# Gated mix of 32-head attention and a dense layer: 23 dense pieces cut into 92 products of 32 rows, ten more summed sets, and a new order

## The chip, the cores and the metric

The kernel runs on one core of one Trainium2 chip. A core has five engines with queues of their own: TensorE (PE in the profile; its weight loads are listed apart as PEld), VectorE (DVE), ScalarE (ACT), GpSimd (POOL) and SyncE (SP), which here only issues transfers and waits. The metric is the device time of one execution in microseconds (us). A run is also profiled once; the profile's span goes from the first instruction to the last one of that execution.

## The reference

One batch, S = 2048 rows of D = 640. The first half is softmax attention with 32 heads of 20 columns, the second a dense layer with 1536 hidden columns and the Mish activation. A sigmoid gate for each row mixes the two.

```python
qkv = (x @ wqkv)                      # to q, k, v of 32 heads, 20 columns each
scores = einsum("bhqd,bhkd->bhqk", q, k) * 20 ** -0.5
o = einsum("bhqk,bhkd->bhqd", softmax(scores), v)
a = o @ wo                            # heads side by side: 2048 x 640

h = x @ w1 + b1                       # 2048 x 1536
b = (h * tanh(softplus(h))) @ w2      # Mish, 2048 x 640

g = sigmoid((x * gate_w).sum(-1))
out = g * a + (1 - g) * b
```

All inputs are bf16.

## The kernel before

**Attention.** Four heads are worked on together: a head's 20 columns are padded to 32 rows, so four heads fill the 128 rows of the array. There are 8 such passes of four heads and 4 chunks of 512 queries, so 32 groups G; a group has 16 key tiles j of 128 keys. A *score unit* is 128 keys by 512 queries of one head: one matmul of 32 rows by 128 columns (`score`, L1073), in the row group of its head (`tile_position=(32 * t_, 0)`). Consecutive score matmuls are called a *visit* here; those in different row groups run side by side. There are 2048 units. 1380 of them get their exponential on ScalarE (`emit_exp`, L1091), one, two or three units an instruction. The other 668 are 167 *sets* of four units (one key tile, all four heads), whose power of two VectorE builds by a multiply and an add into int16 (`power_of`, L586). From that one power a set makes further summands by adding a constant to the int16 bits, which GpSimd does on four at a time as int64 (L616). Of the 167 sets, 155 have three summands, which PE weights and adds (three PV passes); 12 are *summed* (`two` in `d_take`): GpSimd makes a shifted copy, VectorE adds it to the power (`total`, L640), GpSimd shifts once more, and PE has two passes. A *PV pass* (`emit_pv`, L1108) is four matmuls of 128 rows by 21 columns, one in each column group, side by side, onto one PSUM bank (`acc`). There are 834 passes. After its last pass a group is normalised and stored to `o_dram`, from which blocks are loaded back transposed (`load_o`, L923) for the product with `wo`.

**Dense work.** All other products (x@w1, the hidden layer @w2, q, k, v, o@wo) are `Chain`s. A chain holds one PSUM bank from its first piece to its evacuation by VectorE. A *piece* (`product`, L663) takes 128 rows of the contraction: four matmuls of 128 rows by 32 columns, one in each column group, side by side, with 512, 320 or fewer streamed columns. One chain is open at a time (`chain[0]`).

**Order.** The table `ORDER` (L19 to L296) is written out by hand or by a search: each word is one step, and `steps` (L1294 on) runs them in turn. `S n,bank` issues n scores for ScalarE, `x n` the exponential of n, `d G,T,two` takes a set, `D G,j,r,bank` one unit of a set, `p` a GpSimd shift, `V j,i` a PV pass, `C k,bank` opens chain k, `F` runs its next piece, `y k` the VectorE instruction number k, `m` a Mish over half the hidden layer on ScalarE (L871), `q`, `k`, `o`, `b`, `l` loads. Each word puts an instruction at the end of its engine's queue, so the table sets the order on every engine. SyncE's queue holds, in the order in which the words ran, nearly all transfers: the stores that follow an evacuation, the loads of q, k, b and w1, and the transposing loads of `od`. A transfer stands there with the waits for its data, and with those for the buffer that it writes.

PSUM has 8 banks: 7 for scores and chains, one for `acc`.

Of the kernel before, what the change touches and what calls it, by code (L numbers as in the profile page):

```python
# [9 lines left out]
P = 128  # L10
# [9 lines left out]
S2,4 S2,2 C0,6 S2,0 x2 x2 F F F F F C1,5 F y1 y3 C2,4 F x2 y4 C3,5 S2,2 F x2 y5 C4,4 S2,0 F x2 y2 y6 C6,5 S2,2  # L20
x2 F F F F F F F d2,3,0 F F F F F F F F F F F F F C5,6 F F S2,0 S2,3 F F F x2 y7 d0,6,0 y8 y9 x2 y10 y11 y12
C7,2 F F F F F S2,0 x2 S2,5 C8,3 V0,-1 F F F F F F F F F F F F F F F F F F F F y13 y14 y15 x2 V1,-1 S3,0 C9,4
F F F F F S2,5 x3 x2 y16 d0,8,0 y17 y18 y19 d1,5,0 V2,-1 C10,6 V4,-1 S3,0 S2,3 V3,-1 V5,-1 F F F F F x3 x2 y20
C11,5 F S3,0 F F F F F d1,0,0 F F F F F F F D0,15,3,3 x3 D0,15,0,4 F F F F F F F C12,6 F F S3,0 F F F y21 y23
y24 y25 y26 y27 y22 x3 D0,15,2,5 S2,3 x2 y29 d3,4,0 y28 V6,-1 V7,-1 S3,0 C13,5 F F D0,14,3,6 S2,3 F F F x2 q1
y30 y31 x1 x2 C14,0 F F F V9,-1 D0,15,1,6 S2,1 F F F F F F F F F F F S2,3 D0,14,0,5 F V8,-1 y32 x2 q2 y33 x2
D0,14,1,6 S2,1 F F F F F y34 x2 y35 V10,-1 C15,6 S3,3 y36 y37 y38 y39 F F F F F D0,14,2,2 S2,0 F F F F F v0,0
V11,-1 V15,0 y44 y43 y40 p1,1 x3 x2 D1,15,1,5 S3,2 y41 y42 x3 V14,0 V15,1 y45 D1,15,0,6 y46 S2,0 V12,-1 C16,5
F F F F F F S3,2 D1,15,2,6 F F F F p2,7 p3,1 p4,6 d1,2,0 l0 y47 V14,1 V15,2 x2 x3 S2,0 D1,14,0,6 y48 y49 y50
C17,5 V14,2 V13,-1 D1,15,3,2 S2,3 d2,6,0 x2 y51 l1 F F F d1,1,0 x2 y52 D1,14,1,6 S2,0 F F x2 p5,7 S2,2  # L30
D1,14,2,4 x2 p6,8 y53 y54 y55 y56 l2 V0,-1 V1,-1 S2,0 D1,13,0,6 C18,5 F F S3,2 x2 y58 y57 F F F S2,0 D1,13,1,6
V15,0 V15,1 V15,2 V2,-1 x3 y59 l3 y60 x2 D1,12,0,5 y61 C19,6 S3,2 F F F F F F V3,-1 S2,0 D1,14,3,5 F F F F x3
y62 S3,2 x2 l4 y63 p7,8 y64 q3 x1 x2 V4,-1 V5,-1 V14,0 C21,2 D1,13,3,6 D2,15,0,5 S2,0 F d3,5,0 F F F p8,7 y65
y66 x2 S2,3 D1,13,2,6 l5 y67 V14,1 F x2 S2,0 D1,12,3,5 y68 p9,0 V14,2 V13,0 V6,-1 x2 y69 S3,2 D1,12,2,6 p10,8
y70 x1 l6 x2 V7,-1 C20,2 V13,1 S2,0 D1,12,1,5 y71 x2 F F F F F F F F D2,15,3,6 S3,3 F F V13,2 V8,-1 V12,0
p11,7 y72 x3 l7 p12,8 y73 S2,0 D2,15,1,6 y74 y75 d4,0,0 x2 C22,2 V9,-1 V12,1 F D2,14,0,5 S2,3 F F F F
D2,15,2,6 S2,0 F d2,2,0 F F F F y76 x2 l8 y77 x2 y78 S2,4 D2,14,3,3 y79 x2 V10,-1 C23,6 V12,2 F S2,0 D2,14,1,2
F F V11,-1 y80 p13,7 y81 x2 l9 y82 S2,3 D2,13,0,5 F F F F F S2,0 D2,14,2,2 F F p14,1 x2 y84 x2 y83 y85 V15,2
d2,8,1 S2,3 D2,13,3,5 V0,-1 V15,1 V15,0 S2,0 D2,13,1,2 p15,1 x2 e0 p16,7 d2,3,0 x2 y86 y87 y89 y90 e2 V1,-1
V14,0 V14,1 S2,3 D2,12,0,5 C24,2 F F S2,0 D2,13,2,6 F F x2 y91 x2 D2,12,3,3 S2,4 x2 y92 y93 p17,1 F V2,-1 S2,0  # L40
D2,12,1,6 V3,-1 V13,0 V14,2 y94 x2 p18,6 y95 S2,2 x2 D2,11,0,4 C25,5 V13,1 F S2,0 D2,12,2,6 F F y96 y88 y97 x2
D2,11,3,4 S2,2 F F p19,7 y98 x2 S2,0 D2,11,1,6 y99 x2 y101 C26,5 V13,2 V4,-1 D3,15,0,4 S2,2 F F F S2,0
D2,11,2,6 V6,-1 F y102 x2 D3,15,3,4 S2,2 F V5,-1 y100 x2 y103 y105 x2 p20,-1 q4 S2,0 V7,-1 V12,0 x2 d3,6,0
# [12 lines left out]
y154 x2 D4,12,0,6 S2,1 p36,7 x2 y156 V1,-1 V2,-1 C33,5 F S2,3 D4,14,3,0 x2 V15,2 V15,1 S2,1 D4,12,1,6 F F F F
x2 y151 y157 y150 p37,7 S2,3 D4,13,2,0 V14,0 V3,-1 y158 y159 y160 d4,1,0 x2 D4,11,0,6 S2,1 p38,5 y161 y155 x2
V14,1 C35,0 V4,-1 S2,3 D4,13,3,5 F F y162 x2 D4,11,1,6 S2,1 F d5,3,0 F F p39,2 y163 x2 S2,3 D4,12,2,5 y164
V5,-1 V14,2 p40,7 x2 S2,1 D5,15,0,6 y165 V13,1 V6,-1 y166 x2 D4,12,3,0 y167 S3,3 C36,6 F F F D4,11,2,2 S2,0 F
F x3 p41,8 y168 x2 y169 S3,3 V13,2 d5,0,0 C37,2 V13,0 F F D4,11,3,6 S2,0 F d6,4,0 F F x3 x2 d5,2,0 d5,5,0 y170  # L60
y171 p42,-1 p43,7 S2,3 D5,15,1,5 V7,-1 V11,0 V12,0 x2 y172 y173 p44,8 S3,0 D5,15,3,6 V12,1 D5,15,2,5 S2,3
V11,1 V9,-1 V8,-1 V10,-1 V11,2 y174 y175 x3 p45,6 y176 C38,5 S3,0 D5,14,0,6 F F F F F y178 p46,7 x2 x3 y179
y177 C39,0 S2,3 V15,0 V15,1 V0,-1 D5,14,1,6 S2,1 D5,13,0,5 x2 y180 y181 x2 F F F F F y182 S2,3 D5,14,2,6 y183
x2 S2,1 x2 C40,0 D5,13,1,5 V15,2 V2,-1 V1,-1 F y184 y185 D5,14,3,6 S2,3 F F x2 D5,12,0,5 S2,1 y186 y187 F F
p47,1 x2 y188 V3,-1 C41,5 S2,3 D5,13,2,6 V14,0 d6,6,0 F p48,3 x2 y189 D5,12,1,0 S2,1 F F S2,3 D5,13,3,6 F F
y190 y191 x2 S2,0 D6,15,0,2 V4,-1 V14,1 V13,0 y192 p49,7 x2 y193 S3,3 D5,12,3,6 p50,0 y194 x2 V5,-1 D5,12,2,2
S2,0 x3 y195 V13,1 V14,2 V6,-1 V13,2 D6,14,0,5 C42,6 S3,2 p51,8 F F F F q7 q8 y196 x2 p52,1 x3 S2,0 D6,15,2,5
# [12 lines left out]
p66,5 S2,4 D7,13,1,6 d7,0,0 F F F y243 x2 S2,0 D7,13,3,2 V2,-1 V14,0 k2 k3 p68,1 y244 x2 S2,4 D7,13,2,6 V14,1  # L80
V15,2 d8,4,0 y245 y246 x2 D7,12,0,3 p69,6 y247 S3,0 V3,-1 C52,6 F F F F F x1 v3,0 x2 y249 S3,3 D7,12,3,0 C53,6
# [227 lines left out]
def kernel(  # L309
# [12 lines left out]
    nc = tc.nc  # L322
# [326 lines left out]
    def mm_pieces(n, fn):  # L649
        return [(lambda k=k: fn(k)) for k in range(n)]  # L650
# [746 lines left out]
```

## Time and profile before

| | before |
|---|---|
| time, three runs | 684.00, 684.51, 686.26 us (median 684.51) |
| span of the profiled execution | 681.8 us |
| VectorE, L586 (powers), one | 0.682 us, 668 of them |
| VectorE, L640 (total of a summed set), one | 1.210 us, 12 of them |
| GpSimd, L616 (shift), one | 1.042 us, 334 of them |
| GpSimd idle before L616 | 314.2 us |
| granted TensorE clock, mean of the span | 0.999 |

The profiled execution is 2.7 us under the median of the runs. Nearly every time below comes from the profile, so sums are made against its own span of 681.8 us and then set beside the runs. A row of the list of groups has the line, the engine, what is written and read, the shape, the count, and behind the bar the busy time, the mean of one in ns, and the idle time of that engine ahead of such instructions. In a timeline each row is one instruction or a run of equal ones: start, length, engine, line.

### The profile page before, as it was taken

To read this page: it belongs to the slowest core of one execution; us is meant where nothing else is said; L and a number is where in the kernel's file an instruction comes from. 1 tells how busy PE (TensorE), PEld (TensorE's weight loads), DVE (VectorE), ACT (ScalarE), POOL (GpSimd) and SP (SyncE) were. 2 spreads that over 40 slices of the span, in tenths; PEclk is the share of its full clock that TensorE was granted. 3 is DMA by queue.
4 is the path that set the end of the run, shared out by engine and by line. 5 is a ranking of instruction groups with operands and counts; after the bars stand their busy time and mean duration, and the time that the engine had idled before them with its cause. 6 is when DMAs were issued, how large, how long until landed. Compare 5 with 4: busy or idle time off the path is not lost.

```text
span 681.8 us, 24517 instructions
## 1 busy us (share of the span) xinstructions
PE 672.8 (99%) x10355; PEld 234.2 (34%) x10355; DVE 597.3 (88%) x1033; ACT 666.7 (98%) x692; POOL 354.0 (52%) x349
## 2 busy tenths in 40 slices
PE   8999999999999999999999999999999999999997
PEld 4433333323323443333333222222243333333334
DVE  5689989898999889899888988999999988799896
ACT  6999999999999999999999999999999999999996
POOL 5135446454454535565645654456646654466453
PEclk9999999999999999999999999999999999999999
DMA  8444322213312211111231223221232122131221
GB/s 171 118 89 126 81 43 53 53 38 63 89 26 52 49 44 36 26 35 34 43 97 33 43 53 74 64 55 33 56 92 60 21 48 29 41 66 35 60 87 60
DMA packets 128542, 40.47 MB, mean 59 GB/s; under 512 B 94960, under 2 KB 127872, under 8 KB 128432
## 3 DMA queue, kind: packets, MB, share of 16 engines
q1 hardware_dynamic: 126032, 38.29, 25.5%
q8 instruction: 81, 1.33, 0.9%
q10 hardware_dynamic: 2400, 0.62, 0.4%
q14 instruction: 29, 0.24, 0.1%
HBM read 22.29 MB, written 12.78 MB: 51 GB/s over the span
## 4 chain that ended last, share of the span: by engine, by line
PE 89%; ACT 7%; DVE 2%; issue 1%; POOL 0%; DVEq 0%; ACTq 0%
PE Sp L1108 30%; PE Sp L1073 30%; PE Sp L663 29%; ACT E L1091 5%; ACT big L871 2%; DVE T L586 0%; PE Sp L515 0%; PE Sp L1336 0%; DVE T L1151 0%; DVE ot L1353 0%; PE Sp L1217 0%; PE Sp L1123 0%; ACT L1091 0%; PE Sp L1199 0%; ACT big L966 0%
## 5 line engine op out<-in xcount | busy, mean ns | idle before, releaser
L1091 ACT ACTIVATE E<-Sp 128x1024 bf16<-128x1024 f32 (+2 forms) x674 | 634.7, 1127 | 4.4 <-PE Sp L1073 3.7
L616 POOL INT64_ADD T<-T x334 | 344.1, 1042 | 314.2 <-DVE T L586 208.5
L586 DVE TENSOR_SCALAR T<-Sp 128x512 int16<-128x512 f32 x668 | 440.2, 682 | 56.1 <-PE Sp L1073 45.7
L1073 PE MATMUL Sp<-qT,kT 32*128 32x512 bf16 x2048 | 259.5, 384 | 2.9 <-ACT E L1091 1.0
L1073 PEld LDWEIGHTS <-kT 32*128 32x128 bf16 x2048 | 70.1, 91 | 244.9 <-issue 240.4
L1108 PE MATMUL Sp<-E,VA 128*21 128x512 bf16 x1380 | 128.0, 382 | 0.0
L1108 PE MATMUL Sp<-T,VD 128*21 128x512 bf16 x1288 | 117.9, 382 | 0.1
L663 PE MATMUL Sp<-w_sb,big 128*32 128x320 bf16 x1536 | 72.9, 302 | 0.2 <-DVE T L586 0.2
L663 PE MATMUL Sp<-xT,w1t 128*32 128x512 bf16 x960 | 72.2, 382 | 0.0
L1108 PEld LDWEIGHTS <-VA 128*21 128x21 bf16 x2048 | 43.9, 90 | 57.3 <-issue 48.4
L1108 PE MATMUL Sp<-T,VA 128*21 128x512 bf16 x668 | 63.5, 382 | 0.0
L663 PE MATMUL Sp<-xT,ws 128*32 128x512 bf16 x720 | 52.2, 382 | 0.0
L1108 PEld LDWEIGHTS <-VD 128*21 128x21 bf16 x1288 | 29.8, 90 | 38.6 <-issue 32.6
L663 PEld LDWEIGHTS <-big 128*32 128x32 bf16 x1536 | 32.9, 95 | 29.0 <-issue 21.8
L850 DVE TENSOR_SCALAR big<-Sp,b1f 128x512 bf16<-128x512 f32 x48 | 35.6, 741 | 1.8 <-PE Sp L663 1.2
L663 PE MATMUL Sp<-wv,xT 128*32 128x81 bf16 (+2 forms) x960 | 31.0, 257 | 0.0
L663 PEld LDWEIGHTS <-w1t 128*32 128x32 bf16 x960 | 19.8, 95 | 25.4 <-issue 17.4
L752 DVE CAST st<-Sp 128x512 bf16<-128x512 f32 x36 | 24.5, 681 | 2.6 <-PE Sp L663 2.4
L663 PE MATMUL Sp<-wo_sb,od 128*32 128x320 bf16 (+1 forms) x608 | 26.3, 301 | 0.1
L1137 DVE STREAM_TRANSPOSE T<-Sp 128x512 f32<-128x512 f32 x32 | 22.7, 709 | 2.6 <-PE Sp L1108 2.4
L663 PEld LDWEIGHTS <-xT 128*32 128x32 bf16 x960 | 18.8, 96 | 10.8 <-issue 7.7
L663 PEld LDWEIGHTS <-ws 128*32 128x32 bf16 x720 | 15.3, 95 | 19.4 <-issue 12.1
(76 smaller groups left out, 196.8 us busy)
## 6 DMA issues: line engine op xcount, KB each, us to landing
w1t<-in_B_w_dram SPq DMA_DIRECT2D x24, 320.0 KB
q_dram<-st SPq DMA_DIRECT2D x20, 128.0 KB
b_dram<-bt SPq DMA_DIRECT2D x16, 160.0 KB
bl<-b_dram SPq DMA_DIRECT2D x16, 160.0 KB
qT<-q_dram SPq DMA_DIRECT2D x124, 20.0 KB
o_dram<-T SPq DMA_DIRECT2D x120, 20.0 KB
out_dram<-ot SPq DMA_DIRECT2D x15, 160.0 KB
kT<-k_dram SPq DMA_DIRECT2D x28, 80.0 KB
```

Source lines behind the costliest of these rows:

```text
L586: nc.vector.tensor_scalar(out=dst.bitcast(I16), in0=src, scalar1=inv_sqrt_dh * LOG2E * 128.0, scalar2=127.0 * 128.0 + (BETA2 if two else B ...
L616: nc.gpsimd.int64_add(dst[:, :].bitcast(I64), src[:, :].bitcast(I64), n * 0x0001000100010001)
L663: nc.tensor.matmul(out_[k : k + 32], lhsT=lhsT[:, k : k + 32], rhs=rhs, tile_position=(0, k), **kw)
L752: nc.vector.tensor_copy(out=res["st"][:, :], in_=ps[:, :])
L850: nc.vector.tensor_scalar(out=big[:, pair_of(c, ft), (ft % 2) * QC : (ft % 2 + 1) * QC], in0=ps[:, :], scalar1=b1f[:, ft : ft + 1], scalar ...
L871: nc.scalar.activation(v, v, ACT.Mish)
L1073: nc.tensor.matmul(ps_cols, lhsT=kT[p][32 * t_ : 32 * t_ + 32, j * P : (j + 1) * P], rhs=qT[G][32 * t_ : 32 * t_ + 32, :], tile_position=( ...
L1091: nc.scalar.activation(E[:, x : x + n, :], allb[:, k0 : k0 + n, :], ACT.Exp, scale=inv_sqrt_dh,)
L1108: nc.tensor.matmul(acc[32 * t_ : 32 * t_ + DH + 1, :], lhsT=lhsT, rhs=rhs, start=(pv_done[G] == 0), stop=(pv_done[G] == pv_total[G] - 1), ...
L1137: nc.vector.transpose(out=st["T1"][:, :, :].rearrange("p b r -> p (b r)"), in_=acc[:, :])
```

## The change

Besides `ORDER`, the `Chain` class and what runs it are rewritten: a chain now has its own bank, its own count of whole pieces and of parts (`whole`, `top`, `rows`), and several chains can be open at a time (`F k` runs the next piece of chain k). The new step `f k,row` runs one quarter of a piece: the 32 rows of the contraction that lie in row group `row`, as one matmul of 32 rows by 128 columns with all streamed columns, in the row group of a head. It adds to the same bank as the pieces. Four such parts do one piece. So that two parts of one chain never write the bank at once, a `nop` on SyncE stands between them: it waits for the one matmul, and the weight load of the next waits for it.

```diff
 class Chain:
-    def __init__(self, start, due, pieces, evac):
-        self.start, self.due = start, due
-        self.pieces = deque(pieces)
-        self.evac = evac
+    def __init__(self, start, due, n, fn, evac, last=None, cols=512):
...
+        self.fn, self.evac, self.last = fn, evac, last
+        self.n, self.first, self.rows, self.told = n, True, {}, None
+        self.whole, self.top = 0, n
+        self.ps, self.cols = None, cols
+
+    def done(self):
+        return self.whole == self.top and all(len(r) == 4 for r in self.rows.values())
...
-    def product(out_, lhsT, rhs, **kw):
-
+    told = mybir.DependencyInfo(mybir.DependencyClass.Sync, mybir.DependencyReason.DATA)
+
+    def product(ch, out_, lhsT, rhs, row, start=None):
+        if start is None:
+            start, ch.first = ch.first, False
+        if row is not None:
+            r = slice(32 * row, 32 * row + 32)
+            mm = nc.tensor.matmul(
+                out_, lhsT=lhsT[r, :], rhs=rhs[r], tile_position=(32 * row, 0),
+                start=start, stop=ch.done(), skip_group_check=True,
+            )
+            if ch.told is not None:
+                tc.add_manual_dep(mm.ins, ch.told.ins.name, told, reason="parts of one bank")
+            if not ch.done():
+                ch.told = nc.sync.nop()
+                tc.add_manual_dep(ch.told.ins, mm.ins.name, told, reason="parts of one bank")
+            return
         for k in range(0, P, 32):
             nc.tensor.matmul(
-                out_[k : k + 32], lhsT=lhsT[:, k : k + 32], rhs=rhs, tile_position=(0, k), **kw
+                out_[k : k + 32], lhsT=lhsT[:, k : k + 32], rhs=rhs, tile_position=(0, k),
+                start=start, stop=ch.done(), skip_group_check=True,
             )
...
+    def run_part(i, row):
+        ch = chains[i]
+        for k in sorted(ch.rows, reverse=True):
+            if row not in ch.rows[k]:
+                break
+        else:
+            ch.top -= 1
+            k = ch.top
+            ch.rows[k] = set()
+        ch.rows[k].add(row)
+        run(ch, k, row)
...
         "F": run_piece,
+        "f": run_part,
```

One row of the new table, with the chain 166 (half of a row block of the hidden layer @w2) that is spoken of below; its parts are the words `f166`:

```diff
-C166,2 V10,1 V8,-1 V6,-1 S2,0 D30,14,2,5 y936 x2 y937 F F F D30,13,0,6 S2,3 F F V9,-1 x2 p313,2 y938
...
+D30,14,1,6 S2,3 C166,2 F x2 V10,1 d30,1,0 y946 S1,0 p312,-1 D30,14,2,5 x2 S1,1 y947 f166,3 F V8,-1 x2 V10,2
+f166,1 D30,13,0,6 S2,3 F V9,-1 F y948 S2,0 p313,3 D30,14,3,5 f166,2 x2 F x2 F d30,8,0 F y949 F D30,13,1,6 S2,3
+f166,0 F F p314,4 y950 F S1,0 y952 y953 D30,13,2,5 S1,1 V15,0 y954 V15,2 S1,2 b10 p315,0 x2 D30,12,1,6 d30,6,0
```

The table before has 1220 `F`; the new one 1197 `F` and 92 `f`, four for each of 23 chains: 48 with 512 streamed columns and 44 with 320. Each lies in a visit that leaves its row group free: 90 in visits that then have four matmuls, two in visits of three. Of the 167 sets, 22 are summed (12 before), so there are 824 PV passes (834) and ten more L640 totals on VectorE. The 1380 units of ScalarE are 572 pairs, 63 triples and 47 singles (580, 63, 31). There are 641 visits (639) and 640 runs of column-group work between them (637). Two matmuls of one visit share a row group in 15 cases (10). The transfers stay; their order changes. The line numbers move: the score is L1122, the exponential L1140, the PV pass L1157, a piece L702, a part L691, the `nop` L698, the power L618, the total L672, the load of `od` L955.

Two places show what it moves. The first is PE's queue in an early chain of x@w1 (`w1t` the weights, `kT` and `qT` keys and queries, `Sp` PSUM, `T` summands). Before, a visit of three scores is followed by a whole piece:

```order
L1073 LDWEIGHTS kT_82
L1073 MATMUL Sp<-qT_86,kT_82 128x512
L663 LDWEIGHTS w1t
L663 MATMUL Sp<-xT,w1t 32x512
L663 LDWEIGHTS w1t
L663 MATMUL Sp<-xT,w1t 32x512
L663 LDWEIGHTS w1t
L663 MATMUL Sp<-xT,w1t 32x512
L663 LDWEIGHTS w1t
L663 MATMUL Sp<-xT,w1t 32x512
L1108 LDWEIGHTS VA
L1108 MATMUL Sp<-T,VA 21x512
```

Now a quarter of a piece of such a chain stands as the third of four matmuls of a visit:

```order
L1122 LDWEIGHTS kT_82
L1122 MATMUL Sp<-qT_86,kT_82 128x512
L1122 LDWEIGHTS kT_82
L1122 MATMUL Sp<-qT_86,kT_82 128x512
L691 LDWEIGHTS w1t
L691 MATMUL Sp<-xT,w1t 128x512
L1122 LDWEIGHTS kT_82
L1122 MATMUL Sp<-qT_86,kT_82 128x512
```

The piece's column-group work is gone from behind the visit, and its quarter is in the visit, with its own weight load.

The second is SyncE's queue near the end, where the stores of a group's output (`o_dram`) are followed by four transposing loads (`od`), a store of `bt` and one of the output. With the waits of each, before:

```order
L1184 DMA o_dram<-T_0_88 32x16x20 [waits DMAHW6_49]
L923 DMA_TRANSPOSE od<-o_dram 128x512 [waits DMAHW6_49,DMAHW5_49,DMAHW7_49,DMAHW4_49,DMAHW3_49]
L923 DMA_TRANSPOSE od<-o_dram 128x512 [waits DMAHW0_49,PE_49]
L923 DMA_TRANSPOSE od<-o_dram 128x512 [waits DMAHW1_49]
L923 DMA_TRANSPOSE od<-o_dram 128x512 [waits DMAHW2_49]
L902 DMA b_dram<-bt 128x640 [waits DVE_49]
L981 DMA out_dram<-ot 128x640 [waits DVE_49]
L936 DMA bl<-b_dram 128x640
```

And now:

```order
L1233 DMA o_dram<-T_0_88 32x16x20 [waits DMAHW5_49]
L955 DMA_TRANSPOSE od<-o_dram 128x512 [waits DMAHW6_49,PE_49]
L955 DMA_TRANSPOSE od<-o_dram 128x512 [waits DMAHW7_49]
L955 DMA_TRANSPOSE od<-o_dram 128x512 [waits DMAHW0_49]
L955 DMA_TRANSPOSE od<-o_dram 128x512 [waits DMAHW4_49,DMAHW3_49,DMAHW5_49,DMAHW2_49,DMAHW1_49]
L934 DMA b_dram<-bt 128x640 [waits DVE_49]
L1010 DMA out_dram<-ot 128x640 [waits DVE_49]
L968 DMA bl<-b_dram 128x640 [waits PE_49]
```

The first of three loads into the next `od` buffer waits for PE (the last product that reads the buffer's old content) and now heads the four. Between the store `out_dram` and the load `bl` stand the three `nop`s of chain 166, which these rows leave out as they move no data; and on PE the second to fourth part of chain 166 wait for them:

```order
L1157 MATMUL Sp<-T,VD 21x512
L691 LDWEIGHTS big [waits SP_sequencer_49]
L691 MATMUL Sp<-w_sb,big 128x320
L1122 LDWEIGHTS kT_81
L1122 MATMUL Sp<-qT_86,kT_81 128x512 [waits DVE_49]
```

This weight load of the second part (`big` the hidden layer, `w_sb` w2) is ahead of the visit's three scores in PE's queue.

More of the change, by code (lines that the diff above doesn't have):

```diff
@@ L668, in transpose_chain, with piece @@
         c, u = divmod(s, NU)
-        def piece():
-            ps = box["ps"] = bank_tile([P, KT * P], BF16)
+        def piece(ch, k, row):
+            ps = ch.ps = bank_ap(ch.bank, [P, KT * P], BF16)
             for kt in range(KT):
@@ L675, in piece, with evac @@
                 )
[L677 to L678 removed]
+        def evac(ch):
+            ps = ch.ps
             def copy():
@@ L686, in evac @@
             return [copy], None
-        return Chain(start, due, [piece], evac)
+        return Chain(start, due, 1, piece, evac)
     strip_left = {}
@@ L712, in evac @@
             return [(lambda x=x: copy(*x)) for x in parts], lambda: store_top(c)
-        return Chain(start, due, mm_pieces(KT, piece), evac)
+        return Chain(start, due, KT, piece, evac)
     def store_top(c):
@@ L760, in evac @@
             return [copy], done
-        return Chain(start, due, mm_pieces(KT, piece), evac)
+        return Chain(start, due, KT, piece, evac, last)
     def rows_in(kind, p):
@@ L820, in evac @@
             return ops, None
-        return Chain(start, due, mm_pieces(KT * len(sts), piece), evac)
+        return Chain(start, due, KT * len(sts), piece, evac)
+    w1_left = {}
     h_left = [MB * FT // 2] * (NQC // MB)
@@ L861, in evac @@
             return [copy], done
-        return Chain(start, due, mm_pieces(KT, piece), evac)
+        return Chain(start, due, KT, piece, evac, last)
     act_q = deque()
@@ L904, in evac @@
             return [copy], done
-        return Chain(start, due, mm_pieces(FT, piece), evac)
+        return Chain(start, due, FT, piece, evac, cols=HALF)
     wo_sb = [None]
@@ L983, in evac @@
             return [copy], done
-        return Chain(start, due, mm_pieces(n, piece), evac)
+        return Chain(start, due, n, piece, evac, cols=HALF)
     def spread(a, b, n):
@@ L1039, with run @@
     chains.sort(key=lambda ch: (ch.due, ch.start))
-    def run_piece():
-        ch = chain[0]
-        ch.pieces.popleft()()
-        if not ch.pieces:
-            ops, done = ch.evac()
+    def run(ch, k, row):
+        if ch.ps is None:
+            ch.ps = bank_ap(ch.bank, [P, ch.cols])
+        ch.fn(ch, k, row)
+        if ch.done():
+            if ch.last:
+                ch.last()
+            ops, done = ch.evac(ch)
             for f in ops[:-1]:
@@ L1048, in run_piece @@
             dve(ops[-1], done)
+    def run_piece(i=None):
+        ch = chain[0] if i is None else chains[i]
+        ch.whole += 1
+        run(ch, ch.whole - 1, None)
+    def run_part(i, row):
[9 more added lines that the diff above has]
+        run(ch, k, row)
     pool_j = [deque(range(NS)) for _ in range(NG)]
@@ L1291, in begin @@
     def begin(k, bank):
-        chain[0], chain_bank[0] = chains[k], bank
+        chain[0] = chains[k]
+        chains[k].bank = bank
     steps = {
```

677 lines of the change are left out of this document (340 added, 337 removed).

## The prediction

> **What bounds the kernel now.** I read the page's engine line and its chain of waits first, then the list of groups with shapes kept apart, then timelines of TensorE (PE), ScalarE and SyncE.
>
> ```profile
> PE 672.8 (99%) x10355; PEld 234.2 (34%) x10355; DVE 597.3 (88%) x1033; ACT 666.7 (98%) x692; POOL 354.0 (52%) x349
> PE 89%; ACT 7%; DVE 2%; issue 1%; POOL 0%; DVEq 0%; ACTq 0%
> L1073 PE MATMUL Sp<-qT,kT 32*128 32x512 bf16 x2048 | 259.5, 384 | 2.9 <-ACT E L1091 1.0 <-DVE T L586 0.8 <-DVE qT L1236 0.4
> L1108 PE MATMUL Sp<-E,VA 128*21 128x512 bf16 x1380 | 128.0, 382 | 0.0
> L1091 ACT ACTIVATE E<-Sp 128x1024 bf16<-128x1024 f32 x580 | 552.4, 1106 | 3.8 <-PE Sp L1073 3.1 <-ACT E L1091 0.2
> L586 DVE TENSOR_SCALAR T<-Sp 128x512 int16<-128x512 f32 x668 | 440.2, 682 | 56.1 <-PE Sp L1073 45.7
> L640 DVE TENSOR_TENSOR T<-T 128x2048 bf16<-128x2048 bf16 x12 | 14.5, 1210 | 0.6 <-POOL T L616 0.6
> ```
>
> PE carries 89% of the chain and stands idle for little. ScalarE is nearly as full: its pairs waited only 3.8 us. VectorE (88%) waited 56.1 us ahead of its powers, mostly for scores from PE. So PE's order of work sets the end, and ScalarE is a second bound close behind.
>
> What a step costs PE is read from starts, since matmul ends overlap:
>
> ```profile
> 301.02 0.39 PE L1073 MATMUL Sp<-qT,kT 32*128 32x512 bf16 x3
> 301.34 0.62 PE L663 MATMUL Sp<-xT,ws 128*32 128x512 bf16 x8
> 301.89 0.39 PE L1073 MATMUL Sp<-qT,kT 32*128 32x512 bf16 x3
> 303.31 0.39 PE L1108 MATMUL Sp<-T,VA 128*21 128x512 bf16 x4
> 303.52 0.39 PE L1108 MATMUL Sp<-T,VD 128*21 128x512 bf16 x4
> 303.84 0.40 PE L1073 MATMUL Sp<-qT,kT 32*128 32x512 bf16 x4
> 304.17 0.40 PE L1108 MATMUL Sp<-T,VA 128*21 128x512 bf16 x4
> 304.50 0.42 PE L1073 MATMUL Sp<-qT,kT 32*128 32x512 bf16 x3
> 305.72 0.31 PE L663 MATMUL Sp<-w_sb,big 128*32 128x320 bf16 x4
> 242.88 1.12 PE L663 MATMUL Sp<-w_sb,big 128*32 128x320 bf16 x28
> ```
>
> A visit of three costs 0.32 us (301.02 to 301.34), one of four 0.33 (303.84 to 304.17). So a fourth matmul in a free row group is nearly free; that is what the change uses. Two PV passes behind one another start 0.21 apart (303.31, 303.52); I take 0.216, the mean over longer runs. One pass alone between visits takes 0.33 (304.17 to 304.50), so entering and leaving column work costs some 0.11 beside the pass, and a visit of 0.32 is a pass of 0.214 with a switch of 0.107. With 320 columns a piece takes (1.12 - 0.31) / 6 = 0.136, seven pieces being x28 and 0.31 the length of one matmul.
>
> With these, 834 PV passes (180.1), 440 pieces of 512 (95.0), 616 of 320 (83.8), 12.7 of small ones and warm-up, 649 row passes (138.9) and the switches of 639 visits and 637 column runs (139.7) make 650.2. The work begins at 8.47 and the last 8.9 us are the same final products, so 17.4 lies around it:
>
> ```profile
> 8.47 0.60 PE L1073 MATMUL Sp<-qT,kT 32*128 32x512 bf16 x6 [0.44 <-DVE qT L1236]
> 673.38 1.30 PE L663 MATMUL Sp<-wo_sb,od 128*32 128x320 bf16 x32
> ```
>
> 681.8 - 17.4 - 650.2 leaves 14.2 us in which PE waits or stumbles. That is all a better order alone could return.
>
> **The change: work on PE.** Out go ten PV passes and twelve pieces of 512, 22 x 0.216 = 4.75, and eleven pieces of 320, 11 x 0.136 = 1.50; together 6.25. In come seven row passes (two more visits, five more repeated row groups), 7 x 0.214 = 1.50; the switches of two visits and three column runs, 2 x 0.107 + 3 x 0.112 = 0.55; and 87 more visits of four. Those start their successor 4 ns later than visits of three over the whole trace (0.35; by the quoted pair 0.01 each, 0.9). Net **-3.85** (bounds -4.2 and -3.3).
>
> **The parts' waits.** Each of 69 handoffs is PE to SyncE to PE: a part must end (0.38 us by the score row, same form), SyncE must see it, and PE must see SyncE. The nearest row of one hop is ScalarE released by a score:
>
> ```profile
> 99.56 0.39 PE L1073 MATMUL Sp<-qT,kT 32*128 32x512 bf16 x3
> 100.04 1.02 ACT L1091 ACTIVATE E<-Sp 128x1024 bf16<-128x1024 f32 x1 [0.15 <-PE Sp L1073]
> ```
>
> 100.04 - 99.56 - 0.39 = 0.09. Two hops and a step on SyncE make 0.38 + 2 x 0.09 + 0.02, about 0.58. Laying the prices above on the new order, the closest two parts of a chain are 0.65 apart (a visit and one column run; eight pairs), the others 0.70 to 1.84. So 0.58 fits, barely, wherever SyncE stands free. By the same gaps a round trip of 0.8, 0.9 or 1.0 costs 1.9, 4.8 or 9.7 us in all: a steep edge close by.
>
> What SyncE has ahead of each handoff decides the rest. For 65 of the first 66 its queue is through in time by the row lengths below; the fifth has a store ahead that may be late by tenths, which I leave at nothing. The last three, of chain 166, are another matter: four transposing loads, a store of `bt` and a store of the output stand between its first part and its first `nop`.
>
> ```profile
> 543.77 5.08 SPq L923 DMA_TRANSPOSE od<-o_dram  x4
> L923 SPq DMA_TRANSPOSE od<-o_dram x19: 1123/1195/1896, 478.9 to 648.6; - x19
> 604.33 6.18 SPq L923 DMA_TRANSPOSE od<-o_dram  x4
> 603.94 0.34 SPq L902 DMA_DIRECT2D b_dram<-bt  x1
> 618.88 0.36 SPq L981 DMA_DIRECT2D out_dram<-ot  x1
> ```
>
> The first of the four cannot go until the last product out of the old `od` buffer is done. SyncE then needs 0.38 + 0.09 + 5.08 (four at 1.27) + 0.34 + 0.36 + 0.09 = 6.34. PE, from that product to the weight load of the second part, has column runs and visits by turns, by the prices above 0.68 + 0.32 + 0.54 + 0.32 + 0.46 + 0.33 + 0.68 = 3.33 us. It then stands still for **+3.0** us (2.4 with the shortest such load, 1.123; 4.1 with the 6.18 row). Behind that weight load on PE stand the scores that both ScalarE and VectorE need next, so nothing hides it; the third and fourth part find their `nop`s done.
>
> [...]
>
> **The first Mish.** ScalarE is away for 13.0 us, and PE runs against it once:
>
> ```profile
> 230.88 1.28 ACT L871 ACT_TABLE_LOAD   x1
> 232.18 10.44 ACT L871 ACTIVATE big<-big 128x12288 bf16<-128x12288 bf16 x1
> 242.64 1.28 ACT L1091 ACT_TABLE_LOAD   x1
> 245.01 0.39 PE L1073 MATMUL Sp<-qT,kT 32*128 32x512 bf16 x3 [1.01 <-ACT E L1091]
> ```
>
> Before, the scores for the first exponential behind the Mish were issued 1.7 us of PE work after those for the last one ahead of it, and held banks for the whole Mish. In the new order 12.5 us of PE work lie between. I credit the wait, **-1.0** (bound: nothing).
>
> **VectorE and ScalarE.** Ten more totals are 10 x 1.21 = 12.1 us on VectorE. I cost them at nothing: VectorE waits 56.1 us ahead of powers. If that cover fails locally, a power comes late, its bank is freed late, and the next score on PE waits. One such burst of before shows the size:
>
> ```profile
> 515.93 0.72 DVE L1137 STREAM_TRANSPOSE T<-Sp 128x512 f32<-128x512 f32 x1 [0.94 <-PE Sp L1108]
> 516.85 1.16 DVE L640 TENSOR_TENSOR T<-T 128x2048 bf16<-128x2048 bf16 x1
> 518.78 3.14 DVE L586 TENSOR_SCALAR T<-Sp 128x512 int16<-128x512 f32 x5
> 519.52 0.39 PE L1073 MATMUL Sp<-qT,kT 32*128 32x512 bf16 x3 [0.23 <-DVE T L586]
> 520.11 0.73 PE L663 MATMUL Sp<-w_sb,big 128*32 128x320 bf16 x16 [0.20 <-DVE T L586]
> ```
>
> From 515.93 to 518.78 VectorE makes no power, and PE then loses 0.23 + 0.20 (more, inside visits, can't be told apart). The new order has 13 runs of 1.5 us or more of such other work, the old one 8. All twelve totals exposed would be +12, far above anything the row of L640 shows; nothing to +5 x 0.43 = 2.2 is the bound.
>
> ScalarE has eight pairs fewer and sixteen singles more. Inside a run of sixteen (15.04 us) a pair takes 0.94; a single, by its 668 ns against 1106 of a pair, some 0.5:
>
> ```profile
> 515.63 15.04 ACT L1091 ACTIVATE E<-Sp 128x1024 bf16<-128x1024 f32 x16
> L1091 ACT ACTIVATE E<-Sp 128x512 bf16<-128x512 f32 x31 | 20.3, 668 | 0.1
> ```
>
> 16 x 0.5 - 8 x 0.94 = +0.5, covered by ScalarE's waits for PE while PE is the later of the two. It has about 4 us of those to give, so it would cap a larger gain on PE.
>
> **Sum.** -3.85 + 3.0 - 1.0 = -1.85: a span of 680.0, and, the profiled run being 2.7 under the median, **682.6** us beside 684.51.
>
> **The rivals.**
>
> *SyncE does not hold PE* (0.22). Either the loads issue faster there, or PE reaches the place later than laid out. For it: the group of 543.77 is one of few and single loads vary by half. Against it: no row has four of them under 4 x 1.123 = 4.5 us. Then -3.85 - 1.0: 679.7.
>
> *The gain is swallowed* (0.25). VectorE's bursts and ScalarE's narrow margin keep PE's pace: five more bursts at 0.43 (+2.2) on top of the sum: 684.8. For it: both engines near 90% or more, and PE's 14.2 us are already mostly such waits. Against it: VectorE's 56.1 us, and 0.6 us of idle ahead of L640.
>
> *The handoff toll* (0.16): slower. A weight load that waits for a semaphore cannot be taken early, and every part pays for it.
>
> ```profile
> L1073 PEld LDWEIGHTS <-kT 32*128 32x128 bf16 x2048 | 70.1, 91 | 244.9 <-issue 240.4 <-DVE qT L1236 0.6 <-DMA qT<-q_dram 0.5
> 301.02 0.10 PEld L1073 LDWEIGHTS <-kT 32*128 32x128 bf16 x3 [0.42 <-issue]
> ```
>
> The load takes 0.091; 69 of them bare are +6.3, so 682.6 + 6.3 = 688.9. A round trip of 0.95 instead of 0.58 would give the same price by the gaps above; it decides from about 0.85 on. For it: no row shows a hop through SyncE, and the fit is within 0.07. Against it: in the quoted row the load of a visit starts with its matmul (both 301.02), so it is bare at a visit's head today and already in the 0.32.
>
> [...]
>
> **How the numbers follow.** The forecast has 0.37, the three rivals 0.22, 0.25 and 0.16. The forecast's own range is 681.7 (stall 2.4, work -4.2) to 685.3 (stall 4.1, work -3.3, no Mish credit). The range of eight in ten reaches to the second rival's 679.7 less some 2 us for waits that the new order may remove beyond the one counted, and up to the toll's 688.9: **677.5 to 688.5**.
>
> About 0.3% (2.05 us) is what a measurement tells from no change: faster is below 682.46, slower above 686.56. The forecast lies at the edge: 0.16 of its 0.37 faster, 0.20 same, 0.01 slower. No hold: 0.21 and 0.01. Swallowed: 0.05, 0.12, 0.08. Toll: all slower. Faster **0.42**, same **0.33**, slower **0.25**.
>
> **What would show it.** Near 614 us PE's timeline should show one wait of about 3 us ahead of a part of 320 columns, with the `od` loads on SyncE beside it; without it the second rival holds. The wait of 1.01 behind the first Mish should be gone. Waits ahead of other parts, and visits with a part that take 0.4 rather than 0.33, would show the toll. More idle on PE released by L618 or ahead of scores, and less ahead of VectorE's powers, would show the swallowing. The forecast is wrong in its base if PE's starts outside waits do not shrink by some 3.9 us.

## The result: slower by 1.1%

The changed kernel took 691.95 us (five runs, 691.31 to 692.10) where the old one took 684.00 in the same five rounds (683.63 to 686.26). The ratio is 1.0111, with a 95% interval from 1.0098 to 1.0123. The forecast was 682.6 with a range up to 688.5, so the time lies above the range, and on the other side of the old one.

The profiled execution has a span of 690.2 us, 8.4 more than before. In every execution here the time is about 1.8 us above the span, so the old one with a span of 681.8 stands for some 683.6 us, the quick end of its runs; that is why the spans differ by a little more than the medians. Its engine line, and the rows of the parts:

```profile
PE 676.3 (98%) x10315; PEld 241.5 (35%) x10315; DVE 610.5 (88%) x1043; ACT 668.2 (97%) x700; POOL 357.2 (52%) x349
L691 PE MATMUL Sp<-w_sb,big 32*128 32x320 bf16 x44 | 13.8, 314 | 4.3 <-SPq L698 4.3
L691 PE MATMUL Sp<-xT,w1t 32*128 32x512 bf16 x28 | 10.7, 384 | 0.0
L691 PE MATMUL Sp<-xT,ws 32*128 32x512 bf16 x20 | 7.7, 383 | 0.0
```

The reader sees the 92 parts (L691) and ahead of them one idle time of 4.3 us whose releaser is the `nop` on SyncE (L698). The other parts' matmuls show none there. The place is the forecast one, chain 166. TensorE's timeline of the changed kernel around it, and SyncE's transfers beside it:

```profile
634.58 0.30 PE L691 MATMUL Sp<-w_sb,big 32*128 32x320 bf16 x1
634.89 0.32 PE L702 MATMUL Sp<-w_sb,big 128*32 128x320 bf16 x4
635.04 0.39 PE L1157 MATMUL Sp<-E,VA 128*21 128x512 bf16 x4
635.33 0.40 PE L1157 MATMUL Sp<-T,VD 128*21 128x512 bf16 x4
640.03 0.44 PE L691 MATMUL Sp<-w_sb,big 32*128 32x320 bf16 x1 [4.31 <-SPq L698]
640.04 0.61 PE L1122 MATMUL Sp<-qT,kT 32*128 32x512 bf16 x3
640.58 0.46 PE L702 MATMUL Sp<-w_sb,big 128*32 128x320 bf16 x4
```

```profile
632.59 6.23 SPq L955 DMA_TRANSPOSE od<-o_dram  x4
638.87 0.58 SPq L934 DMA_DIRECT2D b_dram<-bt  x1
639.49 0.43 SPq L1010 DMA_DIRECT2D out_dram<-ot  x1
```

The first part starts at 634.58. SyncE is then in the four `od` loads, and after them in two stores until 639.92; the second part starts at 640.03, when all that is issued. The visit at 640.04 then takes 0.54 us to the next start, not 0.32. The windows of the same trace say why (columns: window, busy time and count of PE, PEld, DVE, ACT, POOL, granted TensorE clock, DMA share, GB/s):

```profile
630.00:634.00 4.00, 4.00 (x69) 1.37 (x61) 2.89 (x5) 4.00 (x4) 2.76 (x3) 1.00 0.02 5
634.00:638.00 4.00, 1.72 (x27) 0.59 (x24) 1.41 (x3) 2.25 (x3) 3.21 (x4) 0.94 0.60 78
638.00:642.00 4.00, 1.97 (x20) 0.51 (x20) 1.18 (x2) 1.02 (x1) 0.00 (x0) 0.50 0.48 136
642.00:646.00 4.00, 4.00 (x55) 1.28 (x55) 2.85 (x6) 2.88 (x3) 2.06 (x2) 0.71 0.22 60
646.00:650.00 4.00, 4.00 (x70) 1.36 (x62) 3.25 (x6) 4.00 (x5) 1.04 (x1) 1.00 0.08 28
```

The granted clock falls to 0.50 while TensorE waits and is back only about 644.3, so the first 4.3 us of work behind the wait run at half the clock. By 0.94, 0.50 and 0.71 the clock was at one half for some 6.8 us, from about 637.5 on. That is 1.8 us after TensorE's last matmul, which ended at 635.73. In the trace of e4 below, where the same wait is 3.7 us, the clock falls 3.2 us after the last matmul and again stays at one half for 6.8 us (0.55 from 638 to 642, 0.60 from 642 to 646). So the length of a wait alone does not say here when the clock falls.

To see the rest, take each visit's and each column run's time to the next start and subtract the prices of the prediction. What is left over, summed, is what TensorE waits, also where no row shows it:

| us | before | after |
|---|---|---|
| first visit to last column run | 666.1 | 674.0 |
| left over after the prices | 14.4 | 27.0 |
| of it the wait of chain 166 | - | 4.5 |
| of it the half clock, 640 to 644.6 | - | 1.9 |
| the rest | 14.4 | 20.6 |
| work by the prices | 651.7 | 647.0 |

The priced work shrank by 4.7 us. The waits grew by 12.6: 6.4 in the one place, 6.2 spread over the whole span. The ends grew by 0.5. Together that is the 8.4.

### The profile page after: what moved, and what is told of

It is laid out like the page before. It is cut to its first block, busy times and chain, and to the rows that moved or that the text cites. A ratio compares the mean times of both kernels' runs of the same rounds, so it can differ in the third digit from the quotient of the medians.

```text
span 690.2 us, 24500 instructions
## 1 busy us (share of the span) xinstructions
PE 676.3 (98%) x10315; PEld 241.5 (35%) x10315; DVE 610.5 (88%) x1043; ACT 668.2 (97%) x700; POOL 357.2 (52%) x349
## 5 line engine op out<-in xcount | busy, mean ns | idle before, releaser
L1140 ACT ACTIVATE E<-Sp 128x1024 bf16<-128x1024 f32 (+2 forms) x682 | 636.2, 1086 | 10.8 <-PE Sp L1122 10.0
L618 DVE TENSOR_SCALAR T<-Sp 128x512 int16<-128x512 f32 x668 | 439.4, 684 | 52.3 <-PE Sp L1122 45.4
L1122 PE MATMUL Sp<-qT,kT 32*128 32x512 bf16 x2048 | 263.8, 384 | 3.4 <-DVE T L618 0.8
L1122 PEld LDWEIGHTS <-kT 32*128 32x128 bf16 x2048 | 73.7, 91 | 233.0 <-issue 229.4
L1157 PE MATMUL Sp<-E,VA 128*21 128x512 bf16 x1380 | 127.2, 383 | 0.0
L1157 PE MATMUL Sp<-T,VD 128*21 128x512 bf16 x1248 | 115.9, 382 | 0.1
L702 PE MATMUL Sp<-w_sb,big 128*32 128x320 bf16 x1492 | 79.0, 305 | 0.2
L702 PE MATMUL Sp<-xT,w1t 128*32 128x512 bf16 x932 | 72.6, 383 | 0.1
L1157 PEld LDWEIGHTS <-VA 128*21 128x21 bf16 x2048 | 46.0, 90 | 59.8 <-issue 49.9
L1157 PE MATMUL Sp<-T,VA 128*21 128x512 bf16 x668 | 63.9, 382 | 0.0
L702 PE MATMUL Sp<-xT,ws 128*32 128x512 bf16 x700 | 54.5, 382 | 0.0
L702 PEld LDWEIGHTS <-big 128*32 128x32 bf16 x1492 | 33.9, 96 | 31.3 <-issue 23.7
L1157 PEld LDWEIGHTS <-VD 128*21 128x21 bf16 x1248 | 30.8, 90 | 35.5 <-issue 28.6
L702 PE MATMUL Sp<-wv,xT 128*32 128x81 bf16 (+2 forms) x960 | 37.5, 257 | 0.0
L702 PE MATMUL Sp<-wo_sb,od 128*32 128x320 bf16 (+1 forms) x608 | 29.9, 301 | 0.0
L702 PEld LDWEIGHTS <-w1t 128*32 128x32 bf16 x932 | 20.8, 95 | 25.7 <-issue 18.0
L672 DVE TENSOR_TENSOR T<-T 128x2048 bf16<-128x2048 bf16 x22 | 27.3, 1243 | 0.0
L702 PEld LDWEIGHTS <-xT 128*32 128x32 bf16 x960 | 19.9, 96 | 14.5 <-issue 10.0
```

Of the source, the lines that this page charges most:

```text
L618: nc.vector.tensor_scalar(out=dst.bitcast(I16), in0=src, scalar1=inv_sqrt_dh * LOG2E * 128.0, scalar2=127.0 * 128.0 + (BETA2 if two else B ...
L672: nc.vector.tensor_tensor(out=d[0][:, :], in0=d[0][:, :], in1=d["T"][:, :], op=ALU.add)
L702: nc.tensor.matmul(out_[k : k + 32], lhsT=lhsT[:, k : k + 32], rhs=rhs, tile_position=(0, k), start=start, stop=ch.done(), skip_group_chec ...
L1122: nc.tensor.matmul(ps_cols, lhsT=kT[p][32 * t_ : 32 * t_ + 32, j * P : (j + 1) * P], rhs=qT[G][32 * t_ : 32 * t_ + 32, :], tile_position=( ...
L1140: nc.scalar.activation(E[:, x : x + n, :], allb[:, k0 : k0 + n, :], ACT.Exp, scale=inv_sqrt_dh,)
L1157: nc.tensor.matmul(acc[32 * t_ : 32 * t_ + DH + 1, :], lhsT=lhsT, rhs=rhs, start=(pv_done[G] == 0), stop=(pv_done[G] == pv_total[G] - 1), ...
```

## The experiments

Times are medians; the old kernel ran on the same chip in each group (684.2 to 684.5). e1 to e4 undo parts of the change. e5 and e12 change TensorE's work in the old order. The others take load off VectorE and ScalarE in both orders.

**e1: the `od` loads behind the parts.**

```diff
-y930 V0,-1 V14,0 x2 y932 S2,3 D29,11,1,6 V15,2 V13,0 y933 V2,-1 o3,0,3 C164,6 D30,15,0,5 S1,0 p307,3 x2 S1,1
+y930 V0,-1 V14,0 x2 y932 S2,3 D29,11,1,6 V15,2 V13,0 y933 V2,-1 C164,6 D30,15,0,5 S1,0 p307,3 x2 S1,1
...
-f166,0 F F p314,4
+f166,0 o3,0,3 F F p314,4
```

> The three loads into the next od buffer are issued behind the last part of chain 166 instead of ahead of its first handoff; nothing else moves. Theory (SyncE's queue holds PE for 4.47 us at 634.9, and the granted clock, 0.50 from 638 to 642, costs 1.9 more): both go, 6.3 us less than the changed kernel, 685.6 (685 to 686.4), and the clock stays at 1.00 there. Rival (ScalarE and VectorE are as close behind, so the wait only shows elsewhere): 688 or more. Rival (the handoffs themselves are dear): at most the one wait returns, 687.5 or more.

Measured 685.81 (685.21 to 686.43), ratio to the old kernel 1.0024 (1.0012 to 1.0036). 6.1 us came back, as the theory had it. In its trace the parts of chain 166 follow each other without a wait, and the clock stays:

```profile
634.00:638.00 4.00, 4.00 (x71) 1.45 (x63) 3.26 (x5) 4.00 (x6) 3.84 (x4) 1.00 0.14 45
638.00:642.00 4.00, 4.00 (x70) 1.28 (x62) 3.83 (x8) 4.00 (x5) 2.05 (x2) 1.00 0.29 65
```

So the wait and the clock are most of the loss, but with them gone the new order is still not faster than the old.

**e2: only one of the three loads behind the parts** (`o3,0,2` where `o3,0,3` stood, `o3,2,3` behind `f166,0`).

> Only the third of those loads is moved behind the parts, two stay ahead. Theory (SyncE's issue time is the wait, 1.3 us a load): PE waits about 3.1 us instead of 4.5. If the clock falls only after an idle time longer than that, the loss is 3.1 us beyond the kernel without the wait (688.7); if it falls after any such wait, about 1.9 more (690.5). Rival (the first load's wait for PE, not the number of loads, sets it): no change, 692.

Measured 687.7, 689.81, 690.25 and 691.5, median 690.03. The profiled execution is the one of 687.7. Its wait, on TensorE and on SyncE:

```profile
634.85 0.40 PE L1157 MATMUL Sp<-T,VD 128*21 128x512 bf16 x4
637.55 0.30 PE L691 MATMUL Sp<-w_sb,big 32*128 32x320 bf16 x1 [2.31 <-SPq L698]
637.55 0.39 PE L1122 MATMUL Sp<-qT,kT 32*128 32x512 bf16 x3
```

```profile
632.12 4.22 SPq L955 DMA_TRANSPOSE od<-o_dram  x3
636.44 0.52 SPq L934 DMA_DIRECT2D b_dram<-bt  x1
637.00 0.43 SPq L1010 DMA_DIRECT2D out_dram<-ot  x1
```

One load less takes 2.0 us off the wait (4.31 to 2.31; the theory had 3.1 left), so SyncE's issue time is the cause, and its time per load, 1.4 to 1.6 here, is longer than the 1.27 of the prediction. The mean clock of this execution is 0.999; in the one of 689.81 it is 0.998, in those of 690.25 and 691.5 it is 0.995. So a wait of about this length goes with a lower clock in some executions and not in others; the three took 2.1 to 3.8 us more. How long they waited is not known, and the mean clock is a rough sign: of the five executions of the changed kernel one has 0.998 and the others 0.994 or 0.995, at the same time within 0.8 us.

**e3: all parts whole again.** Each chain's four `f` words are taken out and one `F` with that chain's number put in, next to another of its pieces or between visits.

```diff
-S1,1 y947 f166,3 F V8,-1 x2 V10,2 f166,1 D30,13,0,6 S2,3 F V9,-1 F y948 S2,0 p313,3 D30,14,3,5 f166,2 x2 F x2 F
+S1,1 y947 F V8,-1 x2 V10,2 D30,13,0,6 S2,3 F V9,-1 F y948 S2,0 p313,3 D30,14,3,5 x2 F166 F x2 F
...
-f166,0 F F p314,4
+F F p314,4
```

> All 92 parts are made 23 whole pieces again, each in a column run or between visits of the same chain; order and summed sets as in the changed kernel. Theory (the parts are nearly free but for chain 166): the pieces cost 12 x 0.216 + 11 x 0.136 = 4.1 less 0.4, and 6.3 of wait and clock go: 689.3 (688.6 to 690). Rival (each of the other handoffs costs too, the attribution of waits gives up to 1.3 us): 688. Rival (handoffs dear all over, 0.05 or more each): under 686.

Measured 688.37 (687.65 to 688.78), ratio 1.0063 (1.0048 to 1.0078), a little under the theory's band. It is 2.6 us slower than e1, which differs from it by the parts and that one word of loads. So the parts are worth 2.6 of the 3.75 us that their prices give. Against the old kernel e3 has nearly equal work on TensorE (ten PV passes fewer, seven row passes and some switches more: -2.16 + 1.50 + 0.55), and is 4.1 us slower. The new order with its ten more sums, and with the whole pieces where e3 puts them, costs that much by itself.

**e4: ten totals cut to 64 columns** (their sums are left incomplete).

```diff
-nc.vector.tensor_tensor(out=d[0][:, :], in0=d[0][:, :], in1=d["T"][:, :], op=ALU.add)
+summed.append(0); n = 64 if len(summed) * 5 % 11 < 5 else 4 * QC
+nc.vector.tensor_tensor(out=d[0][:, 0:n], in0=d[0][:, 0:n], in1=d["T"][:, 0:n], op=ALU.add)
```

> Ten of the 22 totals on VectorE add 64 of their 2048 columns (the other columns of those sums are left out), so that VectorE has some 11.5 us less to do while every order stays. PE's waits whose last releaser is VectorE are 6.9 us in the changed kernel and 4.0 before. Theory (the ten more totals make these 2.9): 689 to 690 against 691.95. Rival (the order, not the totals, makes them): within 0.5 us of the changed kernel. Rival (VectorE is the bound): 686 or less.

Measured 691.51 (690.65 to 692.67), with the median among the runs of the changed kernel; the interval of the ratio (1.0093 to 1.0129) is some 1.2 us to either side. VectorE's time on ten of the 22 totals (not exactly the ten that are new) is no visible part of the loss. The theory fell there.

**e5 and e12: TensorE's work in the old order.** In the 23 chains that the change cuts up, one piece each is left out (e5), or done twice (e12). Sets, order and transfers are the old ones.

```diff
     chains.sort(key=lambda ch: (ch.due, ch.start))
+    for k in (24, 45, ..., 166): del chains[k].pieces[-2]                          # e5, and one F less
+    for k in (24, 45, ..., 166): chains[k].pieces.insert(2, chains[k].pieces[1])   # e12, and one F more
```

> The old kernel with one piece left out in each of the 23 chains (12 pieces of 512 columns, 11 of 320; those products are missing from the result), taken from the middle of a column run; order, sets and transfers stay. It takes 12 x 0.216 + 11 x 0.136 = 4.1 us of work off TensorE. Rival (TensorE sets the end, as the prediction had it): 680.3. Theory (ScalarE's and VectorE's pace takes most of what TensorE saves): 682 to 683.5.

> The mirror of the kernel with 23 pieces less: the old kernel with one piece of each of the same 23 chains done twice (those products count double in the result), so 4.1 us more work on TensorE. Theory (the old order is balanced: ScalarE takes back what TensorE saves, but what TensorE adds is paid): 687 to 688.6. Rival (TensorE has 4 us of slack in the old order, ScalarE alone sets the end): 684.5 to 685.5.

e5 took 684.40 (ten runs, 683.54 to 684.60), ratio 0.9995 (0.9986 to 1.0004): 4.1 us less work on TensorE change nothing, where the expectations had 680.3, or 682 to 683.5. e12 took 687.18 (686.78 to 687.49), ratio 1.0047 (1.0030 to 1.0064): 4.1 us more cost 3.0, as its theory had it. The old order stands at a bend.

One of the 23 places shows where the saving goes. TensorE's timeline of the old kernel:

```profile
203.91 0.39 PE L1073 MATMUL Sp<-qT,kT 32*128 32x512 bf16 x3
204.23 0.61 PE L663 MATMUL Sp<-xT,ws 128*32 128x512 bf16 x8
204.78 0.39 PE L1073 MATMUL Sp<-qT,kT 32*128 32x512 bf16 x3
205.10 0.40 PE L1108 MATMUL Sp<-E,VA 128*21 128x512 bf16 x4
```

and of e5 (which runs 0.9 later there from its start on):

```profile
204.81 0.39 PE L1073 MATMUL Sp<-qT,kT 32*128 32x512 bf16 x3
205.13 0.40 PE L663 MATMUL Sp<-xT,ws 128*32 128x512 bf16 x4
205.46 0.60 PE L1073 MATMUL Sp<-qT,kT 32*128 32x512 bf16 x3
205.99 0.40 PE L1108 MATMUL Sp<-E,VA 128*21 128x512 bf16 x4
```

The column run of two pieces took 0.55 to the next start and takes 0.33 with one. The visit behind it took 0.32 and now takes 0.53. The PV pass starts 1.19 us after the first row, then 1.18. The row of that visit is 0.60 long instead of 0.39. No matmul is longer: the last one, of 0.39, ends at 206.06, so it starts at about 205.67, 0.21 behind the first of the visit. As the first still runs then, no idle time is listed. What the second score of the visit waits for is the exponential of ScalarE that is under way, in the old kernel and in e5:

```profile
203.58 1.13 ACT L1091 ACTIVATE E<-Sp 128x1024 bf16<-128x1024 f32 x1
204.48 1.14 ACT L1091 ACTIVATE E<-Sp 128x1024 bf16<-128x1024 f32 x1
```

It ends at 204.71 in the old kernel, ahead of the visit at 204.78, and at 205.62 in e5, where the visit begins at 205.46. ScalarE is where it was but for the 0.9, and TensorE's saving goes into waiting for it. In the whole trace of e5 the left-over of the table above grows from 14.4 to 19.3. Its engine line shows nothing of it:

```profile
PE 672.5 (99%) x10263; PEld 235.3 (34%) x10263; DVE 597.3 (87%) x1033; ACT 666.7 (98%) x692; POOL 354.0 (52%) x349
```

Matching each delayed start with the semaphore it waits for, the delays that end with an exponential or the Mish of ScalarE grow from 8.6 to 12.2 us from the old kernel to e5, and those that end with VectorE from 4.0 to 5.1, of which 1.1 is one wait near the start.

**e6 to e11: the other two engines made faster, in both orders.** VectorE's powers, ScalarE's exponentials, or both, read 256 of 512 columns and write as many 32-bit results, so that every buffer is still written whole; the values are wrong by that. The new order is that of e1, without the one wait.

```diff
-            out=dst.bitcast(I16), in0=src,
+            out=dst.bitcast(mybir.dt.int32), in0=src[..., 0:256],
...
-            E[:, x : x + n, :], allb[:, k0 : k0 + n, :], ACT.Exp, scale=inv_sqrt_dh,
+            E[:, x : x + n, :].bitcast(mybir.dt.int32), allb[:, k0 : k0 + n, 0:256], ACT.Exp, scale=inv_sqrt_dh,
```

> The kernel of the od loads behind the parts (685.8), with every power of VectorE made from 256 of its 512 columns (the values of the VectorE sets are left wrong by that), so that VectorE is never late; order and all other work stay. Beside it the same cut in the old kernel. Theory (the new order loses its gain by waits for VectorE, 7.8 us against 4.0 in the old one): these go and about two thirds of them are kept, 680 to 681, 1 to 2 us under the old kernel with the same cut. Rival (ScalarE's bank rhythm takes the gain): the two differ by +1.6 as without the cut.

> The old kernel with the same cut of VectorE's powers. Theory: the 4.0 us of waits for VectorE go, two thirds of them kept, 681 to 682.5. Rival (VectorE is no matter in either kernel): 684.

> As the new kernel with fast powers, and every exponential of ScalarE too is made from 256 of its 512 columns (the values are left wrong), so that TensorE hardly waits for either: its own work and order alone. Theory (the prices of the sum are right): 664 to 668, and 3.9 to 4.7 us under the old kernel with the same cuts. Rival (visits with parts or the extra switches cost TensorE itself more than 4 ns): less than 2.5 us under it.

> The old kernel with both cuts. Theory: its waits of some 13 us go, save the Mish and the ends, 669 to 672.

> The kernel of the od loads behind the parts with ScalarE's exponentials made from half the columns (values left wrong) and VectorE's powers whole. With both halved it is 3.0 us under the old kernel, with the powers alone 0.3 over it, with neither 1.4 to 1.6 over it. Theory (ScalarE's pace takes the larger part of TensorE's gain, VectorE's the smaller): 1 to 2.5 us under the old kernel with the same cut. Rival (VectorE's lateness alone undoes the gain): not under it.

> The old kernel with the exponentials from half the columns. Theory: between its 672.7 with both cuts and that plus VectorE's waits of 4.0 us: 674 to 677.

Medians in us, old order and new order (e1's):

| | old | new | new less old |
|---|---|---|---|
| as they are | 684.2 | 685.8 (e1) | +1.6 |
| powers halved | 682.8 (e7) | 683.1 (e6) | +0.3 |
| exponentials halved | 677.7 (e11) | 678.3 (e10) | +0.5 |
| both halved | 672.7 (e9) | 669.8 (e8) | -3.0 |

The intervals of e6 and e7 overlap (0.9972 to 0.9991 and 0.9966 to 0.9985), and so do those of e10 and e11. Those of e8 and e9 lie apart (0.9776 to 0.9805, 0.9817 to 0.9846). Only with both engines out of the way is the new order faster. ScalarE alone at its full pace is enough to undo the gain (second row), and VectorE alone too (third row). The expectations that gave the loss to one of the two, first to VectorE (e6), then to ScalarE (e10), both missed. The single times came out above what was expected too: e7 and e9 by 0.3 and 0.7 us over their bands, e8 by 1.8, e11 by 0.7, and the 3.0 us between e8 and e9 are less than the 3.9 to 4.7 that the prices gave. The engine lines of e8 and e9 bear out that TensorE is then what counts:

```profile
PE 661.2 (99%) x10315; PEld 226.5 (34%) x10315; DVE 456.4 (68%) x1043; ACT 437.2 (65%) x700; POOL 357.0 (53%) x349
```

```profile
PE 664.9 (99%) x10355; PEld 225.1 (34%) x10355; DVE 444.4 (66%) x1033; ACT 436.9 (65%) x692; POOL 354.5 (53%) x349
```

No variant here beats the old kernel with the whole computation in it.

## Why the prediction was wrong

**What failed first: "PE's order of work sets the end, and ScalarE is a second bound close behind."** The sum took the whole -3.85 of TensorE's work as time. As work most of it is there: 3.0 us with the other two engines out of the way, 4.7 by the prices of the two profiled executions. As time it is worth nothing in the old order (e5), and 2.6 of the 3.75 that the parts save in the new one (e1 against e3). The engines take turns on the banks, and a score that comes earlier waits for its bank, as in the visit at 205.46 in e5, whose last score starts 0.21 us behind its first. The prediction had 14.2 us in which TensorE waits in its own account and read them as room for improvement; they were the sign that TensorE was already paced.

**The swallowed gain was among the rivals**, with 684.8 and a chance of 0.25, and its price was too small: it gave VectorE's bursts 2.2 us and ScalarE none. e3 puts the new order with its sums at 4.1 us over the old one at about equal work. Which of its many moved words costs that is not settled; e4 only rules out, to within some 1.2 us, VectorE's time on ten totals.

**The wait of chain 166 was right in place and mechanism, and too small.** It was +3.0 with an upper bound of 4.1, and measured 4.5. (The prediction says "near 614 us", but chain 166 stands at 634 to 644; at 614 it is chain 160.) So the rival in which SyncE does not hold PE falls. TensorE's side came out as laid out. SyncE's side took 7.3 us from 632.59 to 639.92 where the sum had 5.78 for the same transfers (5.08 + 0.34 + 0.36), since I took the row of 5.08 for four loads; the row of 6.18 beside it was the nearer one, and the stores took 0.58 and 0.43 rather than 0.34 and 0.36.

**The clock behind it was missing from the sum:** 1.9 us that no term had. The wait of 4.3 us in which TensorE did nothing cost more than itself.

**The first Mish** was credited with 1.0 and gave it: the wait of 1.01 is gone. The waits of the changed kernel list for scores released by ScalarE two short ones in all (columns: total us, times, longest):

```profile
PE Sp L1122 <- ACT E L1140: 0.6, 2, 0.4
PE Sp L691 <- SPq L698: 4.3, 1, 4.3
```

**The handoffs' toll did not come.** Chain 160's first two parts show a handoff that fits:

```profile
613.82 0.39 PE L1122 MATMUL Sp<-qT,kT 32*128 32x512 bf16 x3
613.83 0.30 PE L691 MATMUL Sp<-w_sb,big 32*128 32x320 bf16 x1
614.14 0.46 PE L702 MATMUL Sp<-w_sb,big 128*32 128x320 bf16 x8
614.53 0.39 PE L1122 MATMUL Sp<-qT,kT 32*128 32x512 bf16 x2
614.54 0.30 PE L691 MATMUL Sp<-w_sb,big 32*128 32x320 bf16 x1
```

The second part starts 0.71 after the first, and its visit at once with the scores beside it. The shortest distances in the trace are 0.64 and 0.65 us, at the price of a visit and a column run. The 90 visits of four with a part cost 0.325 to the next start in the changed kernel (median), like the 134 of four scores; with both engines fast (e8) all 92 of them together have no left-over at all once the 4 ns of the fourth matmul are counted. In e1, where no part waits long, the weight loads of seven parts were still released by their `nop`, with 2.8 us of idle time on the loading side (the view of L691 in e1's trace, rows of who ended its idle time, with us and times):

```profile
  SPq L698: 2.8, 7
```

The visits of those seven have 0.3 us left over in all; the rest of those waits lies beside matmuls. So the weight load that waits on SyncE costs at most that here.

**ScalarE and VectorE "at nothing"**: VectorE's own 12 us are hidden, as said (e4). But the cover was counted for VectorE's sum and not for the single bank that comes free late. The traces show it in a rough count, where a left-over is put down to the engine whose semaphore (the counter that the waiting matmul watches) rose less than 0.1 us ahead of a start in it. Those of VectorE are 4.6 us in the old kernel, 9.5 in e3 and 8.9 in e1, with 7.9 in the changed kernel and 7.3 in e4; those of ScalarE 9.6, 10.2 and 12.5, with 13.2 in both others. So the new order alone (e3) mostly adds waits for VectorE, and the parts (e1) add waits for ScalarE. It is a count and no experiment: which words make VectorE late stays open.

So of the 7.9 us between the medians, 6.1 are the one wait and its clock (e1), 4.1 the new order with its sums (e3 against the old kernel), and the parts give 2.6 back (e1 against e3), which makes 7.6. The 0.3 that is left is within the differences between groups of runs. The three differences share their runs and have to add up to the whole, so the sum is no further proof of them.

## What to carry to other kernels

Before a saving on the busiest engine is taken as time, ask what the next instruction on it waits for: leave the work out once and time it, since a busy share of 99% can hold waits between the starts of instructions that overlap (19.3 us left over in e5). A finely balanced schedule can give nothing for less work and still charge for more (4.1 us less gave nothing in e5, 4.1 us more cost 3.0 in e12). When one engine's queue is used to pass a signal between two instructions of another, every transfer ahead in that queue is part of the path (7.3 us of loads and stores here), and a stall of some microseconds on TensorE can be paid again in its clock (1.9 us behind the wait of 4.3).

## What the runs showed of the hardware

A fourth matmul of 32 rows in a free row group, with other weights and another bank than the scores beside it, added 3 ns to a visit of 0.32 us in the changed kernel (median to the next start 0.325 us for the 90 such visits, 0.322 for the 377 of three scores) and 4 ns in e8 (0.325 against 0.321). A signal from TensorE over a waiting SyncE and back fits in 0.64 us from part to part, the matmul of 0.37 included (from 203.84 to 204.48 in the changed kernel). Four transposing loads held SyncE for 5.1 to 6.2 us (5.08 and 6.18 in the old kernel, 6.23 in the changed one), and three for 4.2 in e2 and 3.7 in e1, with nothing else in its queue between them. The granted clock fell to one half 1.8 us into a wait of 4.3 us in the changed kernel, and 3.2 us into one of 3.7 us in e4, and stayed there for 6.8 us both times; after a wait of 2.3 us the profiled execution of e2 kept its clock, while its other three, with a mean clock of 0.995 to 0.998, took 2.1 to 3.8 us longer.
